# One PSUM ring, masked products by pairs, column sums by vector adds, buffers at multiples of 64 bytes and a new order, in a hand-scheduled RWKV-6 plus star-ReLU kernel

## The chip, the cores, the metric

One core of a Trainium2 chip. The metric is the time of one execution in microseconds (us) on the device. The granted clock is the share of its full clock that TensorE had, by the profile's record. Engines are called PE (TensorE), DVE (VectorE), ACT (ScalarE), POOL (GpSimd) and SP (SyncE, which issues the transfers).

## The reference

An RWKV-6 recurrence over 768 steps for 4 batches of 8 heads of 48 columns, then a feed-forward layer with squared ReLU. With s and b scalars:

```python
for t in range(768):
    kv    = k_t outer v_t
    y_t   = r_t @ (state + u*k_t outer v_t)
    state = w_t * state + kv
x = y.transpose(0, 2, 1, 3).reshape(3072, 384)
h = x @ w_in                       # w_in  384 x 2048
g = s * relu(h)**2 + b
out = g @ w_out                    # w_out 2048 x 384
```

The scalar b is moved through the last product: out = s * (relu(h)**2 @ w_out) + b * colsum(w_out). So the **column sums of w_out** are needed before the first output tile can be evicted.

## The kernel before

The recurrence is cut into 24 chunk-batches of 128 steps; two of them make a token tile of the feed-forward layer, so there are 12 tiles. The whole program is one list of words, `ORDER`, by hand: each engine takes its own words in that order and waits by semaphores. `g1T.i` is one of eight steps of the first layer of tile T (six matmuls of 256 columns), `g2T.i` one step of the second (four of 384), `cum`, `tr`, `mt`, `ymm`, `xtr`, `dmm` are the steps of a chunk-batch, `msk` the mask multiply on DVE, `oev` the eviction of an output tile, `+18` eighteen dummy matmuls. The parts that the change touches:

```python
psA = tile_pool(name="psA", bufs=1, PSUM)      # tiles of two banks: cums, masked products
psB = tile_pool(name="psB", bufs=2, PSUM)      # transposes, sums, y
psH = tile_pool(name="psH", bufs=2, PSUM)      # first layer
psO = tile_pool(name="psO", bufs=2, PSUM)      # outputs
par    = const.tile([128, 2], FP32)            # s_bc, b_bc: [128, 1]
cs_sum = const.tile([128, 2, KT], BF16)        # 12 bytes a partition

def mt(n):                                     # masked products of ONE chunk-batch
    ps = psA.tile([128, 2, HP, 128], FP32, name="mt_ps", tag="A")
    for h in range(H):                         # 8 matmuls with 48 rows, two at a time
        ...
def mask(n):                                   # one multiply of 1024 columns on DVE
    ...
def colsum(i):                                 # column sums of one quarter of w_out, on PE
    for ft in range(i * FPP, (i + 1) * FPP):
        for kt in range(KT):
            nc.tensor.matmul(cs[:, kt:kt+1], lhsT=w_out_sb[i][:, ft % FPP, kt*128:(kt+1)*128],
                             rhs=ones[:, 0:1], ...)
def cssplit():                                 # fp32 sum -> two bf16 parts, 128 x 3
    ...
def csspread():                                # 6 matmuls: spread over 128 partitions (csb_ps)
    ...
```

## Time and profile before

| | before |
|---|---|
| median of 3 runs | 187.51 us |
| TensorE busy, granted clock | 97% of the span, 0.999 |
| first h_ps (first layer) | 21.95 us |
| fourth quarter of the first layer | 27.73 us |
| spread of the column sums (csb_ps) | 42.00 us |
| last matmul begins, span ends | 182.3 us, 186.2 us |

A matmul's busy time is modelled; I read PE from **starts**: the time from one start to the next, less the median of that shape, is what I call a stall below, and I sum those over 0.17 us. The kernel before has 0.85 us of them from 20 us to the spread, 0.37 us after it and none after 56 us.

The view by windows of the kernel before (columns: window, its length, busy time of PE, PEld, DVE, ACT and POOL, granted clock, DMA share, GB/s). PE is full, and DVE and ACT have some 3 to 4 us free in 20:

```profile
40.00:50.00 10.00, 9.45 (x114) 6.54 (x115) 8.09 (x14) 8.16 (x17) 5.95 (x9) 1.00 0.95 187
50.00:60.00 10.00, 10.00 (x124) 8.12 (x122) 9.13 (x14) 9.06 (x18) 8.99 (x12) 1.00 1.02 210
60.00:80.00 20.00, 20.00 (x223) 15.64 (x221) 16.27 (x26) 17.31 (x36) 15.49 (x20) 1.00 1.04 211
80.00:100.00 20.00, 20.00 (x222) 16.12 (x221) 16.16 (x24) 17.45 (x35) 15.48 (x20) 1.00 0.81 176
```

### The profile page before, as it was taken

How to read it: one execution, taken by the hardware profiler on the slowest of the kernel's cores; microseconds unless marked ns; L12 is line 12 of the kernel's file. 1: busy time of each engine (PE TensorE's matmuls, PEld its weight loads, DVE VectorE, ACT ScalarE, POOL GpSimd, SP SyncE). 2: the span in 40 equal slices, each digit the busy share in tenths (PEclk: the TensorE clock that was granted, in tenths of full speed). 3: DMA queues.
4: the chain of work that ended last, by engine and by line, in shares of the span. 5: the costliest groups of instructions: out<-in, count | busy, mean ns of one | idle time of the engine just before them, and what ended most of it. 6: DMA issues, size and time to landing. Idle time of an engine off the chain costs nothing.

```text
span 186.2 us, 5073 instructions
## 1 busy us (share of the span) xinstructions
PE 180.6 (97%) x1994; PEld 142.3 (76%) x1994; DVE 131.5 (71%) x220; ACT 142.4 (76%) x277; POOL 103.8 (56%) x141
## 2 busy tenths in 40 slices
PE   7999999999999999999999999999999999999992
PEld 5667888866678788687778877877787877887871
DVE  7478888556799768986987878658788577452231
ACT  3576798797979999769798779974689886678530
POOL 3787840608798695949956265695892167100000
PEclk9999999999999999999999999999999999999999
DMA  6998999888989999999488989999698272000322
GB/s 161 264 308 239 331 318 280 295 180 177 207 190 229 197 221 240 187 213 188 118 199 171 246 164 252 194 186 208 146 212 211 59 184 59 2 0 4 112 99 86
DMA packets 117610, 34.14 MB, mean 183 GB/s; under 512 B 112338, under 2 KB 115539, under 8 KB 117587
## 3 DMA queue, kind: packets, MB, share of 16 engines
q1 hardware_dynamic: 117586, 33.83, 78.3%
q8 instruction: 15, 0.25, 0.5%
q14 instruction: 9, 0.07, 0.1%
HBM read 25.17 MB, written 4.72 MB: 160 GB/s over the span
## 4 chain that ended last, share of the span: by engine, by line
PE 74%; SPq 12%; DMA 7%; DVE 4%; issue 1%; DVEq 0%
PE o_ps L792 31%; PE h_ps L748 29%; SPq L297 8%; DMA wi_st<-in_moe_w_in_dram 5%; PE mt_ps L543 3%; DMA rkt<-in_k_dram 2%; PE y_ps L606 2%; PE xt_ps L699 2%; PE y_ps L597 2%; PE cums L388 2%; PE d_ps L638 1%; DVE gT L773 1%; SPq L719 1%; SPq L305 1%; PE trps L477 1%; SPq L729 1%
## 5 line engine op out<-in xcount | busy, mean ns | idle before, releaser
L748 PE MATMUL h_ps<-xT,w_in 128*128 128x256 bf16 x576 | 77.6, 273 | 0.1
L792 PE MATMUL o_ps<-w_out,gT 128*128 128x384 bf16 (+1 forms) x400 | 75.3, 320 | 0.0
L761 ACT ACTIVATE rh<-h_ps 128x512 bf16<-128x512 f32 x96 | 56.5, 598 | 14.5 <-PE h_ps L748 13.5
L748 PEld LDWEIGHTS <-w_in 128*128 128x128 bf16 x576 | 60.6, 114 | 6.7 <-POOL w_in L880 0.2
L792 PEld LDWEIGHTS <-gT 128*128 128x128 bf16 x400 | 36.2, 98 | 15.3
L771 ACT ACTIVATE gT<-rh 128x512 bf16<-128x512 bf16 x62 | 37.2, 629 | 0.3
L352 POOL TENSOR_TENSOR yd<-vt,cd 128x384 bf16<-128x384 f32 x22 | 20.1, 919 | 30.4 <-DVE cd L346 18.3
L554 DVE TENSOR_TENSOR mt_sb<-mt_ps,tri_strict 128x1024 bf16<-128x1024 f32 x22 | 26.8, 1219 | 4.2 <-PE mt_ps L543 3.8
L323 POOL TENSOR_TENSOR rkp<-rkt 128x384 f32<-128x384 f32 x22 | 24.5, 1112 | 4.7 <-DMA rkt<-in_k_dram 4.6
L329 POOL TENSOR_TENSOR rku<-rkp,u_bc 128x384 f32<-128x384 f32 x24 | 26.0, 1087 | 0.9
L451 DVE TENSOR_TENSOR prd<-rkt,E 128x768 bf16<-128x768 f32 x22 | 23.0, 1045 | 2.8 <-DMA rkt<-in_k_dram 1.6
L803 DVE SCALAR_TENSOR_TENSOR o_sb<-o_ps,s_bc,bconst 128x384 f32<-128x384 f32 (+1 forms) x25 | 14.9, 596 | 10.3 <-PE o_ps L792 10.0
L651 DVE TENSOR_TENSOR x_sb<-y_ps,yd 128x384 bf16<-128x384 f32 x24 | 13.2, 554 | 11.3 <-PE y_ps L606 10.4
L773 DVE TENSOR_TENSOR gT<-rh 128x512 bf16<-128x512 bf16 x34 | 15.8, 482 | 4.9 <-ACT rh L761 4.9
L714 ACT COPY xT<-xt_ps 128x384 bf16<-128x384 bf16 x24 | 11.5, 478 | 6.8 <-PE xt_ps L699 6.8
L346 DVE TENSOR_REDUCE cd<-rku 128x8 f32<-128x384 f32 x24 | 13.0, 543 | 0.9 <-POOL rku L329 0.9
L688 POOL TENSOR_TENSOR st<-stmp,l 128x384 bf16<-128x384 bf16 x16 | 13.1, 829 | 0.7 <-DVE stmp L679 0.7
L1109 PE MATMUL warm_ps<-warm_sb 128*128 128x256 bf16 x74 | 12.2, 309 | 1.1 <-DVE warm_sb L1066 1.1
L424 DVE TENSOR_TENSOR inc<-cums,logw 128x384 f32<-128x384 f32 x16 | 8.9, 554 | 5.5 <-ACT rh L761 1.6
L318 ACT ACTIVATE logw<-wt 128x384 bf16<-128x384 f32 x22 | 11.5, 522 | 1.5 <-DMA wt<-in_w_dram 1.3
L880 POOL CAST vb<-vt 128x384 bf16<-128x384 f32 x14 | 7.4, 536 | 7.6 <-DMA vt<-in_v_dram 4.9
L464 POOL TENSOR_TENSOR l<-E,par 128x8 f32<-128x8 f32 x20 | 7.0, 353 | 6.6 <-ACT E L419 4.7
(96 smaller groups left out, 198.1 us busy)
## 6 DMA issues: line engine op xcount, KB each, us to landing
out_dram<-o_sb SPq DMA_DIRECT2D x23, 192.0 KB, 2.8
wt<-in_w_dram SPq DMA_DIRECT2D x22, 192.0 KB, 3.9
rkt<-in_r_dram SPq DMA_DIRECT2D x22, 192.0 KB, 4.0
rkt<-in_k_dram SPq DMA_DIRECT2D x22, 192.0 KB, 3.8
vt<-in_v_dram SPq DMA_DIRECT2D x22, 192.0 KB, 3.7
wi_st<-in_moe_w_in_dram SPq DMA_DIRECT2D x4, 768.0 KB, 7.5
wo_st<-in_moe_w_out_dram SPq DMA_DIRECT2D x4, 768.0 KB, 7.6
pkt<-in_w_dram SPq DMA_DIRECT2D x1, 384.0 KB, 3.3
```

Of the source, the lines that this page charges most:

```text
L297: nc.sync.dma_start(out=dst, in_=src[bb, :, t0 : t0 + L, :].transpose([1, 0, 2]))
L323: nc.gpsimd.tensor_tensor(out=rkp, in0=c["r"], in1=c["k"], op=ALU.mult)
L329: nc.gpsimd.tensor_tensor(out=rku.rearrange("t h d -> t (h d)"), in0=c["rkp"].rearrange("t h d -> t (h d)"), in1=u_bc, op=ALU.mult,)
L352: nc.gpsimd.tensor_tensor(out=yd, in0=c["v"], in1=c["cd"].unsqueeze(2).to_broadcast([128, H, D]), op=ALU.mult,)
L451: nc.vector.tensor_tensor(out=prd[:, :, :, 0:D], in0=c["rk"], in1=c["E"][:, :, 0:HD].rearrange("t x (h d) -> t x h d", h=H), op=ALU.mult,)
L554: nc.vector.tensor_tensor(out=m.rearrange("s g p t -> s (g p) t"), in0=c["mt_ps"].rearrange("s g p t -> s (g p) t"), in1=(masks[n % 2] if ...
L748: nc.tensor.matmul(ps[:, f, :], lhsT=w_in_sb[ft // FPP][:, kt, :].rearrange("p (m j) -> p j m", j=FPP)[:, ft % FPP, :], rhs=xT[T][:, kt, : ...
L761: nc.scalar.activation(out=rh, in_=hs[T, i], func=AF.Relu)
L771: nc.scalar.activation(out=g, in_=rh, func=AF.Square)
L773: nc.vector.tensor_tensor(out=g, in0=rh, in1=rh, op=ALU.mult)
L792: nc.tensor.matmul(os_[T, k][:, cols], lhsT=gT[T][:, ft, tt * 128 : (tt + 1) * 128], rhs=w_out_sb[ft // FPP][:, ft % FPP, cols], start=(ft ...
L803: nc.vector.scalar_tensor_tensor(out=o_sb[:, cols], in0=os_.pop((T, k))[:, cols], scalar=s_bc, in1=bconst[:, cols], op0=ALU.mult, op1=ALU.add,
```

## The change

Its intent: visit the masked products (48 rows; in the trace of the kernel before a visit takes 0.44 us, 0.21 us more than four pairs of matmuls that start 56 ns apart) half as often, with two chunk-batches' in one visit, take the column sum off PE, let all PSUM users share six banks, and put buffers at multiples of 64 bytes. A new `ORDER` goes with it. The core of the diff (cuts marked, the order text left out):

```diff
-psA, psB, psH (2 + 2 + 2 banks)
+psP = tile_pool(name="psP", bufs=6, PSUM)
-par = const.tile([128, 2], FP32)
+par = const.tile([128, 16], FP32)[:, 0:2]         # the same for s_bc, b_bc, cd, l2, E
-cs_sum = const.tile([128, 2, KT], BF16)
+cs_sum = const.tile([128, 2, d_model], BF16)
 def mt(n):
-    ps = psA.tile([128, 2, HP, 128], FP32)         # one chunk-batch
+    ps = [[psP.tile([128, HP, 128], FP32) for _ in range(2)] for _ in range(2)]   # n and n+1
 ...
-def mask(n):                                       # 1024 columns
+def mask(n, sg):                                   # 512 columns, twice
 ...
-def colsum(i):                                     # 12 one-column matmuls
+def csred(i):                                      # on DVE, in the fp32 staging of w_out
+    for k in (2, 1):
+        eng.tensor_tensor(out=st[:, 0:k], in0=st[:, 0:k], in1=st[:, k:2*k], op=ALU.add)
+def csadd(i):
+    eng.tensor_tensor(out=w_out_cs[0], in0=w_out_cs[0], in1=w_out_cs[i], op=ALU.add)
 def cssplit():                                     # now 128 x 384 instead of 128 x 3
 def csspread():
-    6 matmuls lhsT=cs_sum column, rhs=identity
+    2 matmuls lhsT=ones, rhs=cs_sum[:, x]          # 384 columns each
```

In the new order three loads of the fifth chunk-batch (w, r, k) stand ahead of the last piece of w_in, and 43 squares (34 before) are on DVE. With the ring, the cumulative sums and exponentials of a chunk-batch are also made in halves of one bank each, and one spare buffer of the packed transposes is given up.

## The prediction

Passages that no trace of this case shows are cut, and the cuts marked. The sum is +3.2 - 3.0 = +0.2 us on 187.5, that is 187.7, and the point was put at 187.0. The -2.1 us of the pairing in it is ten times the 0.21 us that a visit takes longer than four times 56 ns. The 0.27 us for the cast of the split is an estimate (a cast of four times the columns took 0.88 us from start to start). In the short paragraph after the four readings of the trace, it is the buffers at multiples of 64 bytes that count as nothing.

> **What bounds the kernel now.** I read the page first, then who waited for whom on TensorE, then the timeline.
>
> ```profile
> PE 180.6 (97%) x1994; PEld 142.3 (76%) x1994; DVE 131.5 (71%) x220; ACT 142.4 (76%) x277; POOL 103.8 (56%) x141
> PE   7999999999999999999999999999999999999992
> DMA  6998999888989999999488989999698272000322
> PE 74%; SPq 12%; DMA 7%; DVE 4%; issue 1%; DVEq 0%
> ```
>
> PE is the only row of nines. Its busy time alone proves little, because ends of matmuls are modelled; the waits and the spacing of starts decide. The view of PE's waits lists these three, all in the first 45 us:
>
> ```profile
> PE warm_ps L1109 <- DVE warm_sb L1066: 1.1, 1, 1.1
> PE cs_ps L831 <- DVE w_out L882: 0.4, 1, 0.4
> PE trps L477 <- DVE prd L451: 0.2, 1, 0.2
> ```
>
> Spacing, in the timeline of PE (start, length, engine, line, operation):
>
> ```profile
> 68.71 0.82 PE L748 MATMUL h_ps<-xT,w_in 128*128 128x256 bf16 x6
> 69.47 0.40 PE L543 MATMUL mt_ps<-RK 48*128 48x128 bf16 x8
> 69.80 0.85 PE L748 MATMUL h_ps<-xT,w_in 128*128 128x256 bf16 x6
> 70.48 0.81 PE L792 MATMUL o_ps<-w_out,gT 128*128 128x384 bf16 x4
> 71.13 0.82 PE L748 MATMUL h_ps<-xT,w_in 128*128 128x256 bf16 x6
> ```
>
> Six matmuls of 256 columns or four of 384 take 0.65 us start to start (70.48 to 71.13), with nothing between. So from about 28 us to the last matmul PE streams, and the time is: when the stream begins, plus its length, plus the tail. The last vector step starts at 182.60 us; the span ends at 186.2 with the store.
>
> The beginning is another stage. Up to 20 us the PE row is filled by 74 dummy matmuls; the limit is the input transfers (DMA row at 8 to 9). The piece of w_in that the fourth quarter of the first layer needs shows it:
>
> ```profile
> 26.21 1.46 POOL L880 CAST w_in<-wi_st 128x1536 bf16<-128x1536 f32 x1 [2.10 <-DMA wi_st<-in_moe_w_in_dram]
> ...
> 27.73 0.85 PE L748 MATMUL h_ps<-xT,w_in 128*128 128x256 bf16 x6
> ```
>
> POOL waits 2.10 us for the fourth piece; its cast ends at 27.67, and the matmul that needs it starts at 27.73. **Transfers, then a cast, gate PE until 27.7 us; after that PE gates itself.**
>
> [...]
> - [...] the masked products (mt_ps, 48 rows) start 0.10 us late (69.36 expected from 68.71 + 0.65, 69.47 seen), and 69.36 to 69.80 is 0.44 us for eight matmuls that run two by two. Four such pairs at the 56 ns that a 128-column transpose takes here would be 0.22. So 0.21 us is lost per visit.
> - [...] 12 one-column matmuls of the column sum take 0.30 us (31.04 to 31.34).
> - [...] The 768-column product prd takes 0.96 us when undisturbed[...].
> - [...] the same product is once 1.52 us.
>
> [...] no row shows a cost that it would remove: I count it as nothing.
>
> **The change, part by part.**
>
> 1. *Masked products of two chunk-batches together.* 24 visits become 12. [...] pairs 0 and 1 lie in the filled beginning, ten lie in the stream: **-2.1 us**. The mask multiply splits into two of 512 columns (0.58 instead of half of 1.22): DVE, beside PE, nothing on the path.
>
> 2. *Column sum.* It leaves PE: four times 0.30 (-1.2), and the spread goes from six matmuls (42.00 to 42.49) to two of 384 columns at 0.163: -0.16. It also removes the gap before the last column sum (0.4 us above).
>
> ```profile
> 42.00 0.65 PE L853 MATMUL csb_ps<-identity,cs_sum 128*128 128x128 bf16 x6
> 42.49 0.33 PE L388 MATMUL cums<-logw,tri_strict 128*128 128x384 bf16 x1
> ```
>
> It comes back on DVE: per piece an fp32 add of 768 columns (0.88 start to start, as prd) and one of 384 (0.47): 1.35, times four; three adds of pieces at 0.47; a split of 0.27 + 0.47. Total 7.5 us, against 0.3 now, all to be done before the spread, hence before the first output can be evacuated.
>
> 3. *New order of transfers.* In the new order three loads more (r, k and w of the fifth chunk-batch) stand ahead of the last piece of w_in, and the first piece stands behind seven loads that now follow it. Successive landings in the trace are 0.9 to 1.1 us apart for a 192 KB load, and the four pieces land at 12.90, 19.96, 24.25 and 26.15. Three loads more put the last piece at about 29.1. Its cast now stands on DVE (0.96, as `w_in` there now), so the fourth quarter starts at about 30.2 instead of 27.7. The first matmul of the first layer, at 21.95 now, I expect at about 23: the first piece lands near 19.9, ACT casts it (1.5), and the two copies of x stand behind that cast in ACT's queue.
>
> 4. *What DVE then has to do, in the program's order*, from the end of that cast (30.15) to the end of the split: one prd 0.88, six squares at 0.35 (2.1), one reduction 0.47, four casts of w_out at 0.88 (3.5), and the 7.5 of part 2: 14.5 us without a gap, to 44.6. Each add that reads what the one before wrote shows its full length rather than the overlapped start to start, some 0.08 each, eight times: 45.3. PE, counted from 30.2 through its own order, would be at the spread at 42.8. **So I expect a new wait of 2 to 3 us on PE, csb_ps behind DVE's split**, and the spread to end near 45.7 instead of 42.5: +3.2 us.
>
> 5. *What is left after the spread.* Now: 182.6 - 42.5 = 140.1 us of stream. Already done by then in the new order: two output steps more (1.30) and one cumulative sum (0.43); still owed: one step of the first layer (0.65) and a masked product (0.43); pairing -2.1; the wait for prd at 44.2 us (0.37 between starts) probably gone. Sum: -3.0.
>
> 6. *Shared PSUM ring.* Six banks for all instead of 2 + 2 + 2 tied ones. PE does not wait for a bank now, so there is nothing to gain in the stream; it only makes the new order possible. Squares move from ACT (62 to 53) to DVE (34 to 43); both have slack.
>
> 7. *Tail.* Two half-width steps and their stores end both; no change, within 0.3.
>
> Sum: +3.2 - 3.0 = +0.2 on 187.5, that is 187.7. Part 4 assumes that DVE's queue never gains on the plan and that the last piece of w_in lands as late as counted; an order made for this program may do a little better, so I put the point at 187.0.
>
> **The rivals.**
> - *The savings come through.* PE loses 2.1 + 1.4 + 0.4 = 3.9 us of work and waits. If the beginning costs nothing, 183.6, just over 2% faster. For it: PE is the bound in 38 of 40 slices. Against it: the beginning is gated by transfers and casts, and the column sum moves onto an engine whose work must end before outputs may leave.
> - *DVE in the beginning takes it all back*, and more [...] (prd once 1.52 instead of 0.96): two or three such hits give 189. For it: 14.5 us of work in a 15 us window. Against it: GpSimd has little to do there (3.4 us busy from 30 to 40 now, by the windows view).
> - *The ring couples what was apart.* Buffers come free in the order of the program, so a mask multiply that is late on DVE holds four of six banks, and PE waits in the stream. ACT is busy 17.3 to 17.6 us in each 20 from 60 to 120 us, so a queue there grows easily. A tenth of a microsecond per pair is 1.2 us; a bad order could cost 3, to 190.
> - *Transfers hidden anyway*: if pieces of w_in land at the 2.0 us of undisturbed ones, the gate is at 28.5 and the time 185.5.
>
> **Range and chances.** The gate is uncertain by 1.2 us, DVE's queue by 1, the stream's new waits by up to 2, nearly all of them independent: 183.8 to 190.2 holds it 8 times in 10. Faster by over 2% (under 183.76) needs the first rival whole: 0.12. Slower by over 2% (over 191.3) needs two bad ones together: 0.08. Within 2%: 0.80.
>
> **What would show it right or wrong.** (1) mt_ps: sixteen matmuls in about 0.65 us, start to next start. (2) No cs_ps; wo_st adds on DVE at 0.96 and 0.55. (3) The last w_in cast on DVE begins near 29; the first h_ps near 23. (4) In PE's waits, csb_ps behind DVE's cs_sum, 2 to 3 us; the spread near 45.5. (5) From there to the last matmul about 137 us. I am wrong if the spread comes at 43 or earlier (then near 184.5), or if PE shows many waits for banks after 50 us (then near 190).

## The result

The changed kernel takes **199.25 us** (median of 4 runs, 199.11 to 199.82), the kernel before 187.28 us. Ratios here are the mean of one kernel's fast runs over the mean of the other's in the same rounds, so not quite the ratio of the quoted medians: 1.0622, 95% interval 1.0573 to 1.0670. It is **6.2% slower**, some 11.7 us, and far out of my range.

The page of the changed kernel: busy times, the clock row and the chain that ended last. PE's busy time stayed (180.6 to 180.5 us, some of it at a lower clock), its share fell from 97 to 91%, the clock row has two slices at 7 and 5 where the kernel before has nines only, and DVE's part of the chain went from 4 to 16%:

```profile
PE 180.5 (91%) x1933; PEld 140.8 (71%) x1933; DVE 152.2 (77%) x264; ACT 136.2 (69%) x264; POOL 111.1 (56%) x145
PEclk9999999997599999999999999999999999999999
PE 55%; DVE 16%; DMA 9%; SPq 9%; ACT 6%; issue 3%; DVEq 0%; ACTq 0%
```

Who PE waited for, changed kernel (us in total, times, longest):

```profile
PE o_ps L792 <- DVE o_sb L803: 2.8, 5, 1.0
PE csb_ps L848 <- DVE cs_sum L840: 2.5, 1, 2.5
PE trps L470 <- DVE prd L443: 2.3, 3, 1.0
...
PE o_ps L792 <- ACT gT L771: 0.9, 1, 0.9
PE h_ps L748 <- DVE mt_sb L554: 0.9, 1, 0.9
```

The wait for cs_sum is the one that I expected. The waits for o_sb are new, and lie in the stream.

PE's timeline of the changed kernel around the spread:

```profile
47.18 0.50 PE L848 MATMUL csb_ps<-cs_sum,ones 128*128 128x384 bf16 x1 [2.47 <-DVE cs_sum L840]
47.95 0.48 PE L848 MATMUL csb_ps<-cs_sum,ones 128*128 128x384 bf16 x1 [0.27 <-DVE cs_sum L841]
48.22 1.48 PE L748 MATMUL h_ps<-xT,w_in 128*128 128x256 bf16 x6
...
51.76 2.32 PE L792 MATMUL o_ps<-w_out,gT 128*128 128x384 bf16 x8
54.01 0.62 PE L542 MATMUL mt_ps<-RK 48*128 48x128 bf16 x16
```

Six h_ps matmuls take 1.48 us, which elsewhere take 0.82; eight o_ps take 2.32 instead of 1.47 (the same group in the run a_keep below). **PE runs at half speed**: the record of the granted clock has 0.5 from 46.67 to 53.50 us. In all 20 traces (two kernels, 18 runs) the clock changes on a grid of 3.41 us, here at 5.71, 46.67, 53.50 and 196.86 us, which are 12, 2 and 42 steps apart; PE's pause had begun at 44.55, between two steps. For each such stretch one can count the columns that PE streamed, as a share of what fits at 384 columns in 0.163 us. From 20 us on, the clock fell after all nine full-speed stretches with a share of at most 0.36 and after none of the 945 others, whose share was 0.39 or more. Here the stretch from 43.26 to 46.67 had 0.10. (Before 20 us it also fell after one of 0.43 and one of 0.48, so the count does not cover everything.)

The mt_ps row shows the pairing at work: sixteen matmuls between 54.01 and the next start at 54.57, where two visits cost 0.86.

DVE in the same kernel, from the last w_in cast to the split:

```profile
29.61 0.98 DVE L873 CAST w_in<-wi_st 128x1536 bf16<-128x1536 f32 x1 [0.20 <-DMA wi_st<-in_moe_w_in_dram]
...
41.76 0.55 DVE L837 TENSOR_TENSOR wo_st<-wo_st 128x384 f32<-128x384 f32 x1
...
44.32 1.40 DVE L837 TENSOR_TENSOR wo_st<-wo_st 128x384 f32<-128x384 f32 x1
...
45.98 1.14 DVE L840 CAST cs_sum<-wo_st 128x384 bf16<-128x384 f32 x1
47.16 0.74 DVE L841 TENSOR_TENSOR cs_sum<-wo_st,cs_sum 128x384 bf16<-128x384 f32 x1
```

The same add takes 0.55 us at 41.76 and 1.40 us at 44.32. What differs in the trace is POOL. It had been idle for 13.34 us, waiting for a load, and begins again in its timeline at 43.11. Its products at 44.31 and 45.74 last until 45.30 and 46.91, and the add and the cast on DVE that begin beside them end only 0.42 and 0.21 us after that. (That both happen together is all that the traces show. In the kernel before, five of the 22 prd took 1.06 to 1.64 us and the others 0.95 to 0.96; POOL was busy beside all five nearly throughout, but also beside the one at 43.74, which took 0.96.)

```profile
43.11 0.77 POOL L871 CAST vb<-vt 128x384 bf16<-128x384 f32 x1 [13.34 <-DMA vt<-in_v_dram]
...
44.31 0.99 POOL L321 TENSOR_TENSOR rkp<-rkt 128x384 f32<-128x384 f32 x1
...
45.74 1.17 POOL L327 TENSOR_TENSOR rku<-rkp,u_bc 128x384 f32<-128x384 f32 x1
```

The view by windows of the changed kernel (columns as above):

```profile
40.00:50.00 10.00, 6.20 (x38) 3.17 (x35) 9.86 (x13) 4.10 (x10) 6.89 (x9) 0.83 1.09 216
50.00:60.00 10.00, 9.40 (x105) 6.55 (x106) 8.17 (x15) 5.19 (x10) 3.10 (x4) 0.83 0.93 192
60.00:80.00 20.00, 19.55 (x228) 15.99 (x226) 19.57 (x32) 17.83 (x36) 18.18 (x23) 1.00 0.65 118
80.00:100.00 20.00, 18.41 (x211) 14.78 (x209) 18.71 (x32) 15.09 (x31) 16.73 (x19) 1.00 0.89 178
```

The clock is 0.83 in both windows from 40 to 60 us. From 60 to 100 us DVE is busy 38.3 us of 40 (32.4 before), and PE has gaps.

So there are **three places**: the pause at the spread (which ends 5.5 us later than before: its last matmul begins at 47.95 instead of 42.43), the half clock, and stalls of 6.1 us after 56 us. From the spread to the last matmul PE needs 146.1 us instead of 139.9.

### The profile page after: what moved, and what is told of

Same layout as the page of the kernel before. It is cut to its first block, busy times and chain, and to the rows that moved or that the text cites. A ratio compares the mean times of both kernels' runs of the same rounds, so it can differ in the third digit from the quotient of the medians.

```text
span 197.3 us, 5006 instructions
## 1 busy us (share of the span) xinstructions
PE 180.5 (91%) x1933; PEld 140.8 (71%) x1933; DVE 152.2 (77%) x264; ACT 136.2 (69%) x264; POOL 111.1 (56%) x145
## 2 busy tenths in 40 slices
DMA packets 117611, 34.16 MB, mean 173 GB/s; under 512 B 112337, under 2 KB 115538, under 8 KB 117586
## 4 chain that ended last, share of the span: by engine, by line
PE 55%; DVE 16%; DMA 9%; SPq 9%; ACT 6%; issue 3%; DVEq 0%; ACTq 0%
PE o_ps L792 25%; PE h_ps L748 19%; SPq L295 6%; DMA wi_st<-in_moe_w_in_dram 5%; DMA wt<-in_w_dram 4%; ACT rh L761 3%; DVE gT L773 3%; DVE o_sb L803 2%; PE mt_ps L542 2%; DVE prd L443 2%; DVE mt_sb L554 2%; PE xt_ps L698 2%; SPq L303 2%; DVE wo_st L830 2%; PE y_ps L605 1%
## 5 line engine op out<-in xcount | busy, mean ns | idle before, releaser
L792 PE MATMUL o_ps<-w_out,gT 128*128 128x384 bf16 (+1 forms) x400 | 73.6, 322 | 3.9 <-DVE o_sb L803 2.8
L748 PE MATMUL h_ps<-xT,w_in 128*128 128x256 bf16 x576 | 74.1, 274 | 2.0 <-DVE mt_sb L554 0.9
L761 ACT ACTIVATE rh<-h_ps 128x512 bf16<-128x512 f32 x96 | 55.1, 598 | 22.4 <-PE h_ps L748 13.8
L771 ACT ACTIVATE gT<-rh 128x512 bf16<-128x512 bf16 x53 | 32.3, 629 | 0.3
L554 DVE TENSOR_TENSOR mt_sb<-mt_ps,tri_strict 128x512 bf16<-128x512 f32 x44 | 27.9, 680 | 4.9 <-PE mt_ps L542 4.8
L773 DVE TENSOR_TENSOR gT<-rh 128x512 bf16<-128x512 bf16 x43 | 25.7, 612 | 6.7 <-ACT rh L761 6.6
L443 DVE TENSOR_TENSOR prd<-rkt,E 128x768 bf16<-128x768 f32 x22 | 24.8, 1126 | 4.3 <-ACT xT L713 2.8
L871 POOL CAST vb<-vt 128x384 bf16<-128x384 f32 x17 | 11.2, 661 | 18.1 <-DMA vt<-in_v_dram 13.3
L412 ACT ACTIVATE E<-cums 128x388 f32<-128x388 f32 (+1 forms) x32 | 15.4, 493 | 7.7 <-POOL rku L327 2.6
L493 ACT COPY RK<-trps 128x1024 bf16<-128x1024 bf16 x7 | 7.1, 1023 | 7.2 <-PE trps L470 7.2
```

The lines of the kernel that those rows point to most:

```text
L412: nc.scalar.activation(out=c["E"][:, x, 0:w], in_=ps[:, 0:w], func=AF.Exp)
L443: nc.vector.tensor_tensor(out=prd[:, :, :, 0:D], in0=c["rk"], in1=c["E"][:, :, 0:HD].rearrange("t x (h d) -> t x h d", h=H), op=ALU.mult,)
L554: nc.vector.tensor_tensor(out=c["mt"][:, sg], in0=c["mt_ps"][sg], in1=(masks[:, n % 2] if packed(n) else tri_strict) .unsqueeze(1) .to_bro ...
L748: nc.tensor.matmul(ps[:, f, :], lhsT=w_in_sb[ft // FPP][:, kt, :].rearrange("p (m j) -> p j m", j=FPP)[:, ft % FPP, :], rhs=xT[T][:, kt, : ...
L761: nc.scalar.activation(out=rh, in_=hs[T, i], func=AF.Relu)
L771: nc.scalar.activation(out=g, in_=rh, func=AF.Square)
```

## The experiments

My theory after the result: the column sum on DVE is the main cause, by its wait, by the clock fall that the wait brings, and by DVE's lateness afterwards. The rival: the new order with more squares on DVE, and the shared ring. The ratio is always to the kernel before; "us over before" is (ratio - 1) x 187.5. The third column answers a question that only arose on the way: where the buffers of the loads begin, modulo 64 bytes, by the addresses in the compiled program.

| run | what it is | load buffers mod 64 | median us | ratio (95%) | us over before |
|---|---|---|---|---|---|
| (changed) | | 0 | 199.25 | 1.0622 (1.0573 to 1.0670) | 11.7 |
| a_keep | changed, PE kept busy in the pause | 0 | 196.03 | 1.0486 (1.0404 to 1.0568) | 9.1 |
| a_cspe | changed, column sum on PE | 32 | 193.24 | 1.0300 (1.0252 to 1.0349) | 5.6 |
| **a_cspe_al** | the same, load buffers at 0 | 0 | 191.04 | 1.0168 (1.0130 to 1.0206) | 3.2 |
| a_fix | a_cspe_al, seven words moved | 0 | 189.28 | 1.0079 (1.0028 to 1.0129) | 1.5 |
| a_best | a_fix, loads moved back | 0 | 189.82 | 1.0089 (1.0030 to 1.0148) | 1.7 |
| a_cspe_sq | a_cspe, squares as before | 32 | 194.25 | 1.0353 (1.0314 to 1.0392) | 6.6 |
| a_cspe_light | a_cspe, 10.5 us less on DVE | 32 | 191.77 | 1.0237 (1.0182 to 1.0292) | 4.4 |
| a_cspe_unpair | a_cspe, pairs taken apart | 32 | 195.66 | 1.0437 (1.0393 to 1.0482) | 8.2 |
| a_cspe_ld | a_cspe, loads moved back, first try | 32 | 199.01 | 1.0598 (1.0551 to 1.0644) | 11.2 |
| a_unpad | changed, small buffers at old sizes | 32 | 200.70 | 1.0693 (1.0650 to 1.0737) | 13.0 |
| b_csdve | before, column sum on DVE | 32 | 196.82 | 1.0472 (1.0399 to 1.0545) | 8.9 |
| **b_csdve_al** | the same, load buffers at 0 | 0 | 195.19 | 1.0371 (1.0311 to 1.0431) | 7.0 |
| b_pad | before, padded, cs_sum left at 12 bytes | 32 | 190.73 | 1.0164 (1.0128 to 1.0200) | 3.1 |
| **b_pad_al** | before, all padded | 0 | 187.75 | 0.9987 (0.9947 to 1.0028) | -0.2 |
| b_ring | order of before on one ring | 32 | 191.22 | 1.0181 (1.0132 to 1.0229) | 3.4 |
| b_ring_al | the same, load buffers at 0 | 0 | 189.31 | 1.0091 (1.0038 to 1.0145) | 1.7 |
| b_ringpair | order of before on one ring, paired | 32 | 203.71 | 1.0860 (1.0809 to 1.0911) | 16.1 |
| b_rp_422 | the same, y products put later | 32 | 197.00 | 1.0501 (1.0451 to 1.0550) | 9.4 |

All are correct but a_cspe_light, which is wrong on purpose.

### The clock, apart from the wait: a_keep

```diff
 def csspread():
     ps = psP.tile([128, d_model], FP32, name="csb_ps", tag="P")
+    for _ in range(20):                       # into the same bank, before the real start
+        nc.tensor.matmul(ps[:, 0:TOK], lhsT=warm_sb[:, 0:128], rhs=warm_sb, start=True, stop=True)
```

> The changed kernel with 20 dummy matmuls of 256 columns put on TensorE directly before the two matmuls of the spread (csb_ps), into the same bank, so that they fill the 2.5 us in which TensorE waits for DVE's cs_sum. The wait itself stays. Theory (the fall of the granted clock to 0.83 in 40 to 60 us follows from that gap and costs by itself about 2.5 us): the clock row stays at 9 in every slice, six h_ps matmuls after the spread take 0.82 again instead of 1.48, and the time falls from 199.25 to about 196.7. Rival (the slow matmuls at 48 to 54 us have another cause, or the saved time is lost again behind a DVE that is late anyway): 199 within 0.5.

```profile
44.64 2.35 PE L849 MATMUL csb_ps<-warm_sb 128*128 128x256 bf16 x20
...
48.05 0.32 PE L853 MATMUL csb_ps<-cs_sum,ones 128*128 128x384 bf16 x1 [0.45 <-DVE cs_sum L842]
48.21 0.81 PE L749 MATMUL h_ps<-xT,w_in 128*128 128x256 bf16 x6
```

In PE's timeline of this run the twenty dummies fill the pause, the spread comes at the same time as in the changed kernel (48.05), and the h_ps group behind it takes 0.81 us instead of 1.48. The ratio falls by 0.0136: **2.6 us, as expected, are the clock with what follows from it**. One of the four executions (198.78 us) had a granted clock of only 0.974; the mean of the other three, at 1.000, lies 3.4 us under that of the changed kernel. From the spread to the last matmul it is 143.0 us instead of 146.1, and the stalls after 56 us are 4.6 us instead of 6.1, with the column sum still on DVE.

### The column sum, from both sides: a_cspe, b_csdve, and what spoiled them

```diff
 # a_cspe: in the changed kernel
-csred, csadd and the wide split and spread
+colsum (48 one-column matmuls), split and spread as in the kernel before
-... csred0 ... csred1 csadd1@D ... csred2 ... csadd2@D ... csred3 ... csadd3@D exp5.0 sq1.3 cssplit
+... exp5.0 sq1.3 colsum0 colsum1 colsum2 colsum3 cssplit
 # b_csdve: in the kernel before, the other way round; csred and csadd directly behind each cast co0 to co3;
 # the packed transposes get one buffer less, to make room
```

> The changed kernel with the column sum back on TensorE (48 one-column matmuls together just before the split, 1.2 us; the wo_st adds on DVE and the wide spread are gone; everything else, order, ring, pairing, squares, as in the changed kernel). Theory (the column sum on DVE is the main cause, by its wait, the clock fall that the wait brings, and the lateness of DVE afterwards): the spread ends near 44 us instead of 48.4, no clock fall, so 199.25 - 4.2 - 2.5 = 192.5, and 190 if the DVE backlog between 60 and 100 us comes from the lateness too. Rival (the new order with nine more squares on DVE, and the shared ring, are the main cause; DVE is busy 19.6 of 20 us from 60 to 80): 195 or more.

> The kernel before with the column sum alone moved to DVE: adds in the fp32 staging directly behind each w_out cast, split over 384 columns, wide spread of two matmuls; order, pools and pairing otherwise as before (one spare buffer of the packed transposes given up to make room). Theory: DVE gets 7.2 us more work between 30 and 42 us, of which it had about 6 us idle, so TensorE waits 1.5 to 4 us at the spread; [...]190 to 194 against 187.3. Rival (the column sum on DVE is harmless, what hurts is the new order): 186 to 187.5.

(From the second: the 2.5 us for a fall of the clock that its range holds were an estimate from the trace of the changed kernel.)

Both went the way of the theory: 6.0 us off in one, 8.9 us on in the other. But the second is over the 190 to 194 that I expected and more than I could account for by its waits, and in both traces the loads were slower than in the two kernels that they were made from (the time of the load queue's packets, in sum, 169 us against 151 and 167 against 146). I did not know why until two runs on the buffers gave nonsense. (In b_csdve a pause of 3.6 us from 36.9 us did not halve the clock: it lies across two stretches of the clock's grid, with shares of 0.48 and 0.42, and the clock stayed at 1. It fell at 49.03, after a stretch of 0.28 at the spread.)

### Buffers and addresses: a_unpad, b_pad, b_pad_al

```diff
 # a_unpad: in the changed kernel
-par, s_bc, b_bc, cd, l2, E padded
+their old sizes
 # b_pad: in the kernel before
-par, s_bc, b_bc, cd, l2, E at their old sizes
+padded as in the changed kernel
```

> The changed kernel with the small buffers (par, s_bc, b_bc, cd, l2, E) back at their old sizes, so not at multiples of 64 bytes. Theory (the 64-byte alignment does nothing for the time): 199.3 within 0.8. Rival (alignment saves something): 200.5 or more.

> The kernel before with nothing but the small buffers (par, s_bc, b_bc, cd, l2, E) at multiples of 64 bytes. Theory (no effect): ratio to the kernel before 1.000 within 0.004. Rival (alignment saves what the run without it in the changed kernel, 200.7 against 199.25 in another call, seems to say): 186.3 or less.

I expected nothing of either. **Taking the padding away cost time in the changed kernel (1.3 us more, intervals just overlapping), and adding it cost time in the kernel before (3.1 us, clearly).** On DVE, ACT and POOL no kind of instruction had grown by more than 0.8 us over all its executions (on PE the half clock stretched h_ps by 2.1 us in b_pad). What both share is in the addresses: in the compiled programs each tile begins at a multiple of 32 bytes, and the small tiles lie ahead of all load buffers. In the kernel before, par, s_bc, b_bc and cs_sum take 32 bytes each, 128 together, so the load buffers happen to begin at a multiple of 64. In b_pad three of them take 64 and cs_sum 32: the load buffers begin 32 bytes past one. The next run differs from b_pad only in cs_sum:

```diff
-cs_sum = const.tile([128, 2, KT], BF16)
+cs_sum = const.tile([128, 2, 16], BF16)[:, :, 0:KT]
```

> The kernel before with all small buffers at multiples of 64 bytes, cs_sum too, so that every buffer begins at one; the run before it (190.73 us) left cs_sum at 12 bytes, which put the load buffers 32 bytes past one. Theory (only the addresses of the load buffers matter, and in the kernel before they already are multiples of 64): 187.4 within 0.5, ratio 0.997 to 1.003, loads at 0.90 to 0.95 us. Rival (padding as such costs): 190 or more.

The line of the main DMA queue on the page (packets, MB, time of its packets as a share of 16 engines' span), first b_pad:

```profile
q1 hardware_dynamic: 117586, 33.83, 87.3%
```

then b_pad_al:

```profile
q1 hardware_dynamic: 117586, 33.83, 81.4%
```

The packets are the same. Their time is 0.873 x 189.7 = 166 us in b_pad and 0.814 x 185.6 = 151 us in b_pad_al, and the ratio is back at 0.9987. Over the 18 traces whose line I have (a_cspe_ld and b_ringpair are not among them) the product lies between 146 and 154 us where the load buffers begin at a multiple of 64, and between 164 and 169 us where they begin 32 bytes past one, also where the other buffers lie the other way round (a_unpad has its o_sb and x_sb at multiples of 64, the kernel before has not). **The address is the cause**; the theory held. (All buffers behind cs_sum move together; that it is the load buffers is read from the packets' time.) In b_pad it brings one wait, for the third piece of w_in, and after that the half clock again (0.87 from 30 to 40 us):

```profile
PE h_ps L749 <- DVE w_in L883: 2.4, 1, 2.4
```

This also explains a_cspe and b_csdve: giving cs_sum another size had moved the load buffers by 32 bytes. So I repeated both with the buffers at their place.

One thing the third column hides: in the changed kernel and a_keep the load buffers begin 64 bytes past a multiple of 128, in the six other runs marked 0 and in the kernel before at a multiple of 128 (by the same addresses). The last section has what the early loads show of it.

### The column sum again: a_cspe_al, b_csdve_al

> The changed kernel with the column sum on TensorE, as in the run that gave 193.24 us, but with cs_sum given 64 bytes, so that the buffers that follow it, those of all loads among them, begin at multiples of 64 bytes as in the changed kernel; in the first run they lay 32 bytes past one. Theory (loads into such buffers are faster: 0.90 us instead of 1.05 us for 192 KB): the last piece of w_in lands 2 us earlier and the time is 190.5 (189.8 to 191.5). Rival (the addresses do not matter, the slow loads of the first run had another cause): 193.2 within 0.6, loads at 1.05 us.

> The kernel before with the column sum alone moved to DVE, as in the run that gave 196.82 us, but with par given 64 bytes, so that the loads write to multiples of 64 bytes as in the kernel before. Theory: the loads take 0.90 to 0.95 us again, and what is left over 187.4 is what the column sum on DVE costs by itself: 193 to 194.5, that is 6 to 7 us, wait and clock fall together. Rival (the address was the main thing in that run): under 190.

Both fell where expected, b_csdve_al by what it adds (7.0 us of 6 to 7), though its median is 0.7 us above the expected 194.5. On the changed kernel the column sum on DVE is worth 1.0622 - 1.0168 = 0.0454, **8.5 us**; on the kernel before, alone, 7.0 us. Up to 0.7 us of the 8.5 may belong to the addresses: the first 164 words of ORDER are the same, yet the fourth quarter of the first layer begins at 30.81 us in the changed kernel and at 30.13 in a_cspe_al. The two who-waits-for-whom lines that matter of b_csdve_al:

```profile
PE trps L476 <- DVE prd L450: 3.4, 1, 3.4
...
PE csb_ps L848 <- DVE cs_sum L840: 1.0, 1, 1.0
```

Here the first wait is not the spread itself: the adds stand in DVE's queue ahead of a prd, and PE waits 3.4 us for the transpose of it. This pause fills one stretch of the clock's grid (share 0.09) and the clock halves from 38.63 to 42.05 us; it halves again from 48.87 to 52.29, behind waits of 1.0 and 0.9 us at the spread (share 0.34). POOL runs beside DVE's work here too: it is busy from 32.99 to 37.17 us, and in DVE's timeline the cast and the pair of adds beside it take 1.76 and 2.73 us, where later ones take 0.95 and 1.55:

```profile
33.05 1.76 DVE L873 CAST w_out<-wo_st 128x1536 bf16<-128x1536 f32 x1
34.84 2.73 DVE L830 TENSOR_TENSOR wo_st<-wo_st 128x768 f32<-128x768 f32 x2
```

In a_cspe_al the spread's last matmul begins at 44.29, 3.7 us before that of the changed kernel, and from there to the last matmul it is 141.6 us instead of 146.1: 8.1 of the 8.5 us. Of these last 4.4 us a_keep got 3.0 by the clock alone. The stalls after 56 us are 4.6 us in a_keep as here, so they do not come from the column sum; of the lateness in my theory a_keep shows one wait, 1.7 us for a prd right behind the spread.

### What is left: ring, pairing, loads, DVE's load

**The ring.** The order of before was carried over to the ring of six, with words put later only where a bank would not be free, the column sums in one lump:

```diff
-psA, psB, psH
+psP (six banks), masked products still one chunk-batch at a time
-g11.1 ... colsum0 ... colsum1 ... colsum2 ... colsum3 ... cssplit
+... colsum0 colsum1 colsum2 colsum3 cssplit; dmm4, ymm4, tr5 some steps later
```

> The order of the kernel before on the changed structure without the pairing: one ring of six banks, 64-byte buffers, column sum on TensorE in one lump, masked products one chunk-batch at a time as before. Theory (one shared ring costs nothing by itself as long as the order was not made worse): 187 to 188.5. Rival (the ring alone couples the engines, and explains the 203.7 of the run with ring and pairing): 191 or more, with TensorE waiting for banks held by mask multiplies or sums.

> The order of before on one ring of six banks, unpaired, column sum on TensorE in one lump (191.22 us with load buffers 32 bytes past a multiple of 64), now with them at multiples of 64. Theory (after 52 us that run had no stall over 0.2 us; its 3.7 us came from the late loads and from the lump): 188 to 189.5. Rival (the ring costs): 191.

1.7 us over before, with the sums and masks in halves included. After 56 us this trace has one stall, of 0.23 us; its losses lie at 27 to 50 us, around the lump and the moved words. **The ring itself costs nothing in the stream.** (The first of the two, at 191.22, met the rival's number; half of its 3.4 us goes with the addresses.)

**The pairing, under an order that was not made for it.**

```diff
-mt4 (8 matmuls) ... mt5 (8 matmuls)
+(nothing)       ... mt4 (16 matmuls, where mt5 was), masks behind it
```

> The order of the kernel before carried over to the structure of the changed kernel: one ring of six banks, masked products of two chunk-batches together, 64-byte buffers, column sum on TensorE in one lump before the split. What is not in it: the new order and the DVE column sum. Theory (ring and pairing are sound): pairing saves 2.1 us, the wait for the last w_out cast at the column sum of 0.4 us may stay: 185 to 185.8. Rival (the shared ring couples DVE's mask multiplies to TensorE's banks): 188 or more, with TensorE waits on mt_sb or h_ps after 50 us.

203.71 us, a clear miss. Who PE waited for in b_ringpair:

```profile
PE y_ps L605 <- DVE mt_sb L554: 6.2, 18, 0.4
PE xt_ps L698 <- DVE x_sb L650: 4.0, 5, 1.6
```

The y product stood right behind the products whose mask multiplies it needs. So I put it four steps later:

> As the run with ring and pairing under the order of before, but with the dependent y products of each pair (from the ninth chunk-batch on) put at least four MLP steps (2.6 us) behind the masked products, and the x transposes two steps behind those. In the 203.7 us of that run TensorE waited 18 times for mt_sb (6.2 us) and 5 times for x_sb (4.0 us). Theory (the pairing saves 0.21 us per pair, but it puts four mask multiplies of 0.6 us in a row on DVE before the first y product may start, so its worth depends on the distance in the order): the mt_sb waits nearly go and the time is 186 to 190. Rival (the pairing itself is the loss): over 195.

197.00: better by 6.7 us, with 1.9 us of mt_sb waits left, but now 3.6 us in which PE waits for output evictions that stand behind the four masks in DVE's queue. The expected 186 to 190 was missed even if 1.7 to 3.3 us, what the addresses cost in four other pairs of runs, are put down to them. A change of structure can only be judged with an order made for it; these two runs say nothing against the pairing.

**The pairing, under its own order.**

```diff
-mt4 ...                      # chunk-batches 4 and 5
+mt4 ... two steps ... mt5    # and so on for ten pairs; 0 and 2 left together
```

> The changed kernel with column sum on TensorE (193.24 us), with the masked products of the ten pairs in the stream taken apart again: the second of each pair two MLP steps behind the first, its mask multiplies behind it. Theory ([...]): 2.1 us more, 195.3. Rival (the pairing is paid back by four mask multiplies in a row on DVE): 193.3 or less.

(The 0.21 us per pair: the theory is that the pairing saves them, ten times.)

From 1.0300 to 1.0437: 2.6 us lost, in an order in which only the second halves were put two steps later, 2.0 of them visible between the spread and the last matmul (142.1 to 144.1 us). **The pairing is worth about what I had worked out for it** (2.1 us).

**DVE's load in the stream.**

```diff
 # a_cspe_sq, tiles 2 to 8
-squares: 21 of 56 on DVE
+squares: 16 of 56 on DVE, as before
 # a_cspe_light (wrong on purpose)
-prd over 8 heads, cd over 48 columns
+prd over 4 heads, cd over 24 columns
```

> The changed kernel with column sum on TensorE (193.24 us), and besides the squares of the token tiles 2 to 8 given to the engines that had them before (fewer on DVE: 14 of 56 instead of 20). Theory (what is left over the kernel before, 5.7 us, is in good part DVE's queue between 60 and 160 us, where it is 19.7 of 20 us busy): the waits for o_sb shrink and the time falls to 190 to 191.5. Rival (the order fixes what waits for what, and ACT at 17.9 of 20 us becomes the late one): 193 or more, with waits on ACT's rh or gT.

> Wrong results on purpose: the changed kernel with column sum on TensorE (193.24 us), and the product prd (22 times, 1.13 us) computed for half of the heads, the reduction cd (22 times, 0.54 us) over half of its columns, so that DVE has about 14 us less to do in the same order, with the same waits. TensorE, ACT, POOL and the transfers do what they did. Theory (after 50 us TensorE stands still about 5 us in all because DVE's queue is full and runs late): nearly all of that goes, 188 to 189.5. Rival (the order itself, or ACT, holds TensorE, whatever DVE's load): 192 or more.

(The expectation miscounts: it is 21 and 16 squares, not 20 and 14.) Both went against my theory. With squares back on ACT the waits for o_sb shrink from 2.2 to 0.5 us as expected, but others grow (xt_ps behind x_sb from none to 2.6, h_ps behind xT from 1.6 to 2.0), and the time rises by 1.0 us. In a_cspe_light DVE's busy time fell by 10.5 us (140.2 to 129.7), not by the 14 that I had expected, and the stretch from the spread to the last matmul shrinks by only 1.1 us (142.1 to 141.0), and 4.3 us of stalls after 56 us remain of 5.2. (Its total is blurred by a wait of 2.7 us for xT at 23 us, with the half clock behind it.) **That DVE is full is not the main thing that holds PE**; the next run tries the order in which it takes its work.

**The order.** The mapping of stalls to words showed, in a_cspe_al, seven places where an eviction, a sum or a square stood behind work that nobody needed yet. Moving just these:

```diff
-oev2.0 sup8 sq3.2 relu3.5 mul11 ... oev2.1      +oev2.0 oev2.1 sup8 sq3.2 relu3.5 mul11
-relu4.4 inc14 cd12 oev3.1 ... yev10             +relu4.4 oev3.1 yev10 inc14 cd12
-exp17.0 inc17 ... cd15 ... oev4.0               +exp17.0 oev4.0 inc17
-cum22.0 inc21 exn21 oev6.1                      +cum22.0 oev6.1 inc21 exn21
-g28.7 ... cd22 yev20 g19.5 oev8.1               +g28.7 oev8.1
-sq9.4@A cd23 relu9.6 yd23 sq9.3                 +sq9.4@A sq9.3 cd23 relu9.6 yd23
```

> The changed kernel with column sum on TensorE and aligned load buffers (191.04 us), and seven instructions moved up in the order of their own engine, past work that is not urgent: the evictions of the second half of output tile 2, 3, 6 and 8 and of the first half of tile 4, one sum y, and one square on ACT. No engine gets less to do. Theory (the waits of 4.6 us after 56 us are a matter of the order: an eviction that could run stands behind a product that nobody needs yet): most of the waits go, 187 to 188.5. Rival (DVE and ACT are overloaded there, so a wait removed at one place comes back at another): 190 or more.

1.0168 to 1.0079: 1.7 us, with no engine doing less. Of the seven stalls five went or shrank to 0.2 us; one came back in another form and one stayed, both as x transposes that wait for the sums y, and a new one of 0.56 us appeared at 144 us. The waits for output evictions are gone from the list:

```profile
PE xt_ps L697 <- DVE x_sb L649: 1.4, 2, 0.7
```

Stalls after 56 us are 2.4 us instead of 4.6. From the spread to the last matmul it is now 139.2 us, under the 139.9 of the kernel before for the first time. The interval of the ratio is 187.9 to 189.8 us; it reaches into the expected 187 to 188.5 and not to the rival's 190. About half of the effect that I hoped for came.

**The early loads.** The first try put them behind the pieces of w_in, with the w load of the same chunk-batch:

```diff
-... load4.1 load4.2 load3.3 li0 load4.0 li1 li2 li3 lo0
+... load3.3 li0 li1 li2 li3 load4.0 lo0 small2 load4.1 lo1 load4.2
```

> The changed kernel with column sum on TensorE (193.24 us), with the three loads w, r, k of the fifth chunk-batch again behind the four pieces of w_in, as in the kernel before (and the rk products, the prd and the transposes of that chunk-batch moved behind accordingly). Theory (the gate of the last w_in piece delays all that follows): the fourth quarter of the first layer starts 2 to 2.5 us earlier and the time is 191. Rival (what comes early is lost again behind DVE in the stream): 193 within 0.6.

A miss, at 199.01, and one of my making: the pieces of w_in did land earlier (the third at 24.65 instead of 28.86 us, the fourth at 26.74), but the logarithm of w stands in ACT's queue ahead of the second copy of x, and now waited for its load. ACT's timeline, the two copies with the logarithm between them:

```profile
24.64 0.49 ACT L712 COPY xT<-xt_ps 128x384 bf16<-128x384 bf16 x1
28.64 0.52 ACT L315 ACTIVATE logw<-wt 128x384 bf16<-128x384 f32 x1 [3.51 <-DMA wt<-in_w_dram]
29.07 0.46 ACT L712 COPY xT<-xt_ps 128x384 bf16<-128x384 bf16 x1
```

PE waits 3.1 us for that second copy.

The second try left the w load at its place:

```diff
-load4.1 load4.2 load3.3 li0 load4.0 li1 li2 li3 lo0
+load3.3 li0 load4.0 li1 li2 li3 load4.1 load4.2 lo0      # rkp4, rku4, mul4, cd4 later too
```

> As a_fix, and the loads of r and k of the fifth chunk-batch behind the four pieces of w_in instead of ahead of them, with the products that need them moved behind as well. Theory (three loads ahead of the last w_in piece delay the start of the stream, and nothing takes that back later): the first h_ps at 22 to 23, the fourth quarter of the first layer at 28 to 28.5 instead of 30.1, and 185 to 186.5 us, under the kernel before. Rival (the products that now come later stop DVE or the transposes at 32 us): 187 or more.

The first h_ps begins at 22.94 instead of 23.80 and the fourth quarter at 29.02 instead of 30.09, so half of what I hoped. The spread is no earlier, 45.30 against 44.25, for two reasons. The four pieces of w_out and the load behind them land up to 2 us later (the last piece at 39.02 instead of 37.06 us), and PE stalls 0.9 us at 39.4 us for a logarithm of that load. And in the profiled execution the clock halved from 42.69 to 46.10 us: the stall and the 48 one-column matmuls of the column sum lie in one stretch of the grid (share 0.36). The five other executions had a clock of 0.998 or more, and their mean is 189.43 us, against 189.24 for a_fix. **Putting the loads back gains a microsecond at the start and nothing at the end**; how it is lost without the half clock I have not traced. The interval of 189.82 overlaps that of a_fix. No version beat the kernel before.

## Why the prediction was wrong

It named the right places and sized two of them far too small.

- *Pairing (-2.1 us).* Right: 16 matmuls in 0.56 us, 2.6 us when undone.
- *Column sum on DVE, a wait of 2 to 3 us at the spread.* The wait was right: 2.47 + 0.27. The time of it was wrong: I said that the spread would end near 45.7, its last matmul began at 47.95. **The failed term is DVE's queue**: I counted the last adds and the split at 0.27 to 0.55 us each, as if undisturbed, on the grounds that "GpSimd has little to do there". POOL woke up at 43.11, and the add at 44.32, the cast and the subtraction took 1.40, 1.14 and 0.74 us. DVE was done at 47.9 instead of 45.3. I had named this rival and given it 189. That the wait still came out at 2 to 3 us is luck: PE, too, reached the spread late, at 44.55 instead of 42.8.
- *What follows from that wait.* **This step is missing altogether.** "+3.2 us" is what PE loses by standing still. That the pause also halves the clock, for 6.8 us, is not in the sum; it cost 2.6 us (a_keep).
- *From the spread to the last matmul, about 137 us.* (The working counted to the last vector step at 182.6; the last matmul of the kernel before begins at 182.3.) Failed: 146.1. With the clock kept up it is 143.0 (a_keep), and the rest is stalls: 4.6 us after 56 us, with the column sum on DVE (a_keep) as without it (a_cspe_al). I took it that an engine with slack in the mean (16 of 20 us) keeps up with any order, and let "the stream's new waits" cost up to 2 us. The runs showed that the waits depend on which word stands before which: seven words were worth 1.7 us, 10.5 us of DVE work about 1.
- *Loads ahead of w_in: the fourth quarter of the first layer, which I called the gate, at 30.2, first h_ps near 23.* Nearly right: 30.81 and 24.10. But taking the cost back gained nothing at the end (a_best).
- *64-byte buffers count as nothing.* For before against after this is right (b_pad_al: 0.9987), but by luck. The load buffers of the kernel before happen to begin at multiples of 64; with the wide cs_sum and without the padding they would not have, and that costs 1.3 us here and 3.1 us in the kernel before. "No row shows a cost that it would remove" was true of the profile's page, and the address is not on that page.
- *Shared ring: nothing in the stream.* Right (b_ring_al).

The sum, by ratios: column sum on DVE 8.5 us (2.6 of it the clock; up to 0.7 may be the addresses), order of DVE and ACT 1.7 us, and 1.5 us left over, in which the later start of the stream (spread at 44.25 instead of 42.43 us) and the remaining 2.4 us of stalls stand against the 2.6 us that the pairing earned. I have not separated these last ones by a run of their own.

## What to carry to other kernels

Work that is moved off the bounding engine must be looked at in the queue where it lands: who stands behind it there, and what else wakes up meanwhile (an add took 1.40 us beside POOL, 0.55 before). The pause on PE cost twice here, 2.5 us for itself and 2.6 us by the clock, which stayed at half for 6.8 us (in other runs for 3.4); whether the clock fell went with how little PE had streamed within one stretch of the clock's 3.41 us grid (a share of at most 0.36, against 0.39 or more), and dummy matmuls into a bank that is overwritten anyway took away the second part (a_keep). Before comparing two versions, compare the addresses of the buffers that loads write to: a 12-byte constant in front of them was worth up to 3 us and spoiled the sizes of several experiments before I saw it.

## What the traces show of the addresses and of the clock

- The packets of this kernel (112337 of 117611 under 512 bytes) took 164 to 169 us in sum where the load buffers began 32 bytes past a multiple of 64, and 146 to 154 us where they began at one; a kernel gained 3.3 us by it (b_pad to b_pad_al).
- From 20 us on, the clock halved after each of the nine full-speed stretches of 3.41 us in which PE streamed at most 0.36 of the columns that fit, and after none of the 945 with 0.39 or more.
- Multiples of 64 bytes were not all alike. In the changed kernel and a_keep, whose load buffers begin 64 bytes past a multiple of 128, packets of 192 bytes took 18.3 to 18.9 ns between 8 and 14 us; in the seven kernels that begin at a multiple of 128, 15.0 to 15.7. The first 384 KB loads landed 1.5 us apart in the changed kernel, 1.2 in the kernel before. Two programs are too few to call this a rule, and after 30 us the difference is gone (15.3 ns in the changed kernel, 15.5 in the kernel before, from 30 to 60 us).
